# Window attention, forward and backward, on one core: the turn of P moved from TensorE to VectorE, three slots for turned y and h, and a new order of the first steps

## The chip, the cores and the metric

The kernel runs on one core of a Trainium2 chip. The metric is the time of one execution on the device in microseconds (us); for a set of runs the median is given. Engines: PE (TensorE, matmuls), DVE (VectorE), ACT (ScalarE), POOL (GpSimd) and SP (SyncE). POOL and SP do almost nothing here but issue DMAs.

## The reference

```python
def _fwd_reference(x, wqkv, wo):            # x (1, 256, 256, 384) bf16, C = 384
    # x is cut into 32 x 32 windows of 8 x 8 = 64 positions: xw (1024, 64, 384)
    qkv = xw @ wqkv
    q, k, v = qkv[..., :C], qkv[..., C:2*C], qkv[..., 2*C:]
    p = softmax(einsum('bqc,bkc->bqk', q, k) * C ** -0.5)
    o = einsum('bqk,bkc->bqc', p, v) @ wo
    return o                                 # windows put back in place

def reference(x, wqkv, wo, grad_out):
    out, vjp = jax.vjp(_fwd_reference, x, wqkv, wo)
    return (out, *vjp(grad_out))             # out, dx, dwqkv, dwo
```

## The kernel before

The weights are multiplied together first, so that q, k and v are never formed: A = scale wq wk^T and B = wv wo, with their transposes AT and BT. Then for each window y = x A, the scores are y x^T, and P is their softmax; h = grad_out BT, and h x^T is the gradient of P, from which D, the gradient of the scores, follows. out is P x B. dx is made of D x AT, D^T y and P^T h. For the weights only two sums over all windows are needed, x^T V with V = D^T x, and x^T W with W = P^T grad_out; an epilogue multiplies them by the weights.

**Units.** A quad is 8 windows, 512 positions, kept as four tiles t of 128 partitions with two windows (64 partitions each, w = 0, 1). There are NQ = 128 quads, and `step(n)` is called once for each. The order inside a step is written by hand: each engine runs its instructions in the order in which the code issues them, and waits by semaphores where data or a buffer isn't ready. A step works on several quads at once: n (attention products and outputs), n+1 (turn of P), S = n+2 (scores and softmax), A = n+3 (projections), n+4 (turns of inputs), n+5 (loads).

**Parts of a step, with their lines.** All matmuls go through a helper (L85), and ACT and DVE evictions from PSUM through `ev` (ACT L89, DVE L91).

- `md(n)`: x times the turned P and D (tile TT), 48 matmuls in 64x64 pieces, evicted to MD.
- a dW block (`Block.mms`): x^T V or x^T W for 24 tiles (six quads) and 128 of the 384 rows. In the two-bank form (banks 3 and 4) each tile takes four 64x64 matmuls of 384 columns, in the one-bank form (bank 3) one 128x128 matmul. Tiles 0 to i1 and i1 to i2 use two banks, i2 to the end one. `blk.add` adds a bank to ACC on DVE (L309) and so frees it.
- `attn2(n, h)`: V, W and two of the three parts of dx for half a quad, 64x64 pieces; it reads P and D (PB), x, grad_out and the turned y and h (YH). V and W are evicted to VW, with a slot for each of NVW quads. The steps before the first dW block is there (n = 0, 1, 2, called early) use `attn_vw` and other banks.
- `dxs(n, t)`: the third part of dx; `dxs_ev` evicts it to DXS on ACT, and POOL stores it (L277).
- `scores(S)`: both score products into bank 4, from HYS, in which `stack` (DVE, L134) has put y and h side by side.
- `chain0`, `chain2`, `chain3`: the softmax and its gradient. chain0 (DVE, L153 and L155) subtracts the maximum into SS, chain2 (ACT, L159) is the exponential, chain3 (DVE, L163 to L170) gives P and D in PB; it reads bank 4 again (L167), and after that the bank is free. UM is a buffer of chain3.
- `proj(A, 0)` and `proj(A, 1)`: y and h of a later quad, held transposed, evicted to YHT. They read the turned inputs XT and DOT.
- `outs(n, t0)`: out from MD and B, evicted to OS on ACT, stored by POOL (L219).
- `turn_p(n+1)`: P and D turned within each window: 16 PE transposes of 64x64 (L179) into bank 7, and one DVE copy to TT (L180).

**Turns and loads.** SP's queue issues, in this order in each step: the turns by DMA of x and grad_out of quad n+4 (`turn_in`, L111, to XT with three slots and DOT with two), the load of grad_out of quad n+5 (L107), and the turns of y and h of quad n+2 (`turn_yh`, L115, to YH with NTOK = 2 slots). POOL's queue loads x of quad n+5 (L103) and stores both outputs. ACT's queue issues DMAs at the start and the end only.

A prologue forms A, B, AT and BT (`wprod`), and brings quads 0 to 2 to where step 0 needs them.

Of the kernel before, what the change touches and what calls it, by code (L numbers as in the profile page):

```python
# [11 lines left out]
BF16 = mybir.dt.bfloat16  # L12
# [4 lines left out]
def kernel(  # L17
# [18 lines left out]
    NQ = (H // 16) * NQC  # L36
    scale = float(C) ** -0.5
    GQ = 6
    NX, ND, NXT, NDT, NYH, NTOK, NVW = 13, 5, 3, 2, 3, 2, 9

    def cut(q):

# [28 lines left out]
    SS = sb.tile([P, 4, 64], F32, name="SS")  # L71
    PEX = sb.tile([P, 4, 64], F32, name="PEX")
    TM = sb.tile([P, 4, 64], F32, name="TM")
    UM = sb.tile([P, 4, 64], F32, name="UM")
    ST = sb.tile([P, 4, 4], F32, name="ST")
    ACC = sb.tile([P, 2 * CK, C], F32, name="ACC")
    ident = sb.tile([P, P], BF16, name="ident")
# [6 lines left out]
    def mm(out, lhsT, rhs, start, stop):  # L84
        PE.matmul(out, lhsT=lhsT, rhs=rhs, start=start, stop=stop, skip_group_check=True)  # L85
# [28 lines left out]
    def turn_yh(n, a):  # L114
        SP.dma_start_transpose(out=YH[:, n % NTOK, a, :, :],  # L115
                               in_=YHT[:, n % NYH, a, :, :].rearrange("p m t -> p (m t)"))
# [14 lines left out]
    def stack(n, a, m0, m1):  # L131

        dst = HYS[:, 4 * m0:4 * m1, 0::3, :] if a == 0 else HYS[:, 4 * m0:4 * m1, 1:3, :]
        DVE.tensor_copy(out=dst, in_=YHT[:, n % NYH, a, m0:m1, :].rearrange("p m (t w k) -> p (m t) w k", w=2, k=64))  # L134
# [16 lines left out]
    def chain0(n):  # L151
        for w in range(2):
            DVE.tensor_reduce(out=ST[HALF[w], 0, :], in_=sd(w, w), axis=AX.X, op=ALU.max)  # L153
        for w in range(2):
            DVE.tensor_tensor(out=SS[HALF[w]], in0=sd(w, w),  # L155
                              in1=ST[HALF[w], 0, :].unsqueeze(2).to_broadcast([64, 4, 64]), op=ALU.subtract)

    def chain2(n):
        ACT.activation(out=PEX[:], in_=SS[:], func=ACTF.Exp)  # L159
# [10 lines left out]
        DVE.tensor_tensor(out=pb[:, 0], in0=TM[:], in1=UM[:], op=ALU.subtract)  # L170

    def turn_p(n):
        bb = PS[:, 7, 256:512].bitcast(BF16)
        for t in range(4):
            for a in range(2):
                for w in range(2):
                    r = slice(64 * w, 64 * w + 64)
                    o = t * P + a * 64
                    PE.transpose(bb[r, o:o + 64], PB[r, n % 2, a, t, :], ident[r, r])  # L179
        DVE.tensor_copy(out=TT[:, n % 2, :, :, :].rearrange("p t a k -> p (t a k)"), in_=bb)  # L180

    def pturn(dst, src, banks, engs):

# [88 lines left out]
    def dxs_ev(n, h, eng):  # L272
        ev(eng, DXS[:, n % 2, 2 * h:2 * h + 2, :].rearrange("p a c -> p (a c)"),
           PSF[:, DXB + 2 * h * C:DXB + 2 * h * C + 2 * C])
        for t in (2 * h, 2 * h + 1):
            for w in range(2):
                POOL.dma_start(out=img(out_1, n, t)[8 * w:8 * w + 8], in_=DXS[64 * (1 - w):64 * (1 - w) + 64, n % 2, t, :])  # L277

    class Block:
# [8 lines left out]
        def mms(self, banks, i0, i1):  # L288

            if i0 == 0:  # L290
                self.banks = len(banks)
            for i in range(i0, i1):
                q, t = self.tiles[i]
                s0, s1 = i == 0, i == len(self.tiles) - 1
                xs, vs = (q % NX) * 4 + t, (q % NVW) * 4 + t
                if len(banks) == 1:
                    mm(PS[:, banks[0], 0:C], X[:, xs, self.ma * P:(self.ma + 1) * P], VW[:, vs, self.which, :], s0, s1)
                    continue
                for hh in range(2):
# [42 lines left out]
    def wprod(dst, lt, r0, sc):  # L342
        for mo in range(CK):
            o = PS[:, bank[0] % 6, 0:C]
            bank[0] += 1
            for m in range(CK):
                mm(o, lt[:, m, mo * P:(mo + 1) * P], r0[:, m, :], m == 0, m == CK - 1)
            if sc:
                ACT.activation(out=dst[:, mo, :], in_=o, func=ACTF.Copy, scale=scale)
            else:  # L350
                DVE.tensor_copy(out=dst[:, mo, :], in_=o)

    def step(n):
        S, A = n + 2, n + 3
        doS, doA = S < NQ, A < NQ
        early = not todo
        if n + 4 < NQ:
            turn_in(n + 4, 0)
            turn_in(n + 4, 1)

        md(n)
        if early:
            if doA:
                proj(A, 0, (3, 4, 0, 5), (ACT, ACT, ACT, DVE))
            if n + 1 < NQ:
                turn_p(n + 1)
            attn_vw(n, 0, 0)
            vw_ev(n, 0, 0, ACT)
            attn_vw(n, 1, 2 * 512)
            attn_vw(n, 2, 2 * 512 + 2 * C)  # L370
            vw_ev(n, 1, 2 * 512, DVE)
            vw_ev(n, 2, 2 * 512 + 2 * C, ACT)
            attn_vw(n, 3, 0)
            vw_ev(n, 3, 0, ACT)
            if doS:
                stack(S, 0, 0, 3)
                stack(S, 1, 0, 3)
            if n + 5 < NQ:
                load_x(POOL, n + 5)
        else:  # L380
            blk = todo.pop(0)
# [48 lines left out]
        outs(n, 0, (5, 6), ACT)  # L430
        outs(n, 2, (4, 7) if early else (0, 1), ACT)
        outs_st(n)
        if not early and doA:
            proj(A, 1, (7, 2, 4, 3), (ACT, ACT, ACT, DVE))
        elif not doA:
            fill(7, 2, 4)

    def gate(ap):
# [2 lines left out]
    with tc.manual_schedule():  # L441
# [33 lines left out]
        wprod(A_sb, wT[:, 0:CK], wT[:, CK:2 * CK], True)  # L475
# [6 lines left out]
        wprod(BT_sb, wo_sb, wT[:, 2 * CK:3 * CK], False)  # L482
        stack(0, 0, 0, 3)
        pturn_in(1, 0, (6, 7), (ACT, ACT))
        proj(0, 1, (4, 5, 0, 1), (ACT, DVE, ACT, DVE))
        stack(0, 1, 0, 3)
        turn_yh(0, 1)
        turn_in(2, 1)
        pturn_in(1, 1, (6, 7), (ACT, ACT))
        scores(0)  # L490
        chain0(0)
        proj(1, 0, (0, 1, 2, 3), (ACT, ACT, ACT, ACT))
        turn_yh(1, 0)
        chain2(0)
        chain3(0)
        proj(1, 1, (5, 6, 7, 0), (ACT, ACT, ACT, ACT))
        turn_yh(1, 1)
        stack(1, 0, 0, 3)
        stack(1, 1, 0, 3)
        wprod(AT_sb, wT[:, CK:2 * CK], wT[:, 0:CK], True)  # L500
        scores(1)
        chain0(1)
        wprod(B_sb, wT[:, 2 * CK:3 * CK], wo_sb, False)
        turn_in(3, 0)
        turn_in(3, 1)
        turn_p(0)
        chain2(1)
        chain3(1)
        proj(2, 0, (0, 1, 4, 5), (ACT, ACT, ACT, ACT))
        proj(2, 1, (6, 7, 0, 4), (ACT, ACT, ACT, ACT))  # L510
        for n in range(NQ):
            step(n)
            if n == NQ - 3:
# [78 lines left out]
```

## Time and profile before

| | |
|---|---|
| median of 7 runs | 1965.92 us (1956.68 to 1990.76) |
| profiled execution, its own time | 1962.67 us |
| its span | 1960.8 us |
| PE, DVE, ACT, POOL busy | 99%, 69%, 69%, 58% of the span |
| step 0 begins | 38.0 us |
| granted TensorE clock | 0.999 |
| SP's turns of y and h, from issue to landing | 7.3 us (median) |
| the same for x, grad_out | 6.6 us, 8.9 us |

A row of the profile's groups or timeline names the line, the engine, the operation, output<-inputs, the tile (partitions x elements) and the time; in brackets stands the engine's idle time before it and what ended it. PE's 99% is time in which some matmul was under way; matmuls overlap, so the share alone doesn't say how fast they follow each other. The chain of waits is followed back from the last instruction: where it stays on PE, nothing but PE's own order held it up.

### The profile page before, as it was taken

To read this page: it belongs to the slowest core of one execution; us is meant where nothing else is said; L and a number is where in the kernel's file an instruction comes from. 1 tells how busy PE (TensorE), PEld (TensorE's weight loads), DVE (VectorE), ACT (ScalarE), POOL (GpSimd) and SP (SyncE) were. 2 spreads that over 40 slices of the span, in tenths; PEclk is the share of its full clock that TensorE was granted. 3 is DMA by queue.
4 is the path that set the end of the run, shared out by engine and by line. 5 is a ranking of instruction groups with operands and counts; after the bars stand their busy time and mean duration, and the time that the engine had idled before them with its cause. 6 is when DMAs were issued, how large, how long until landed. Compare 5 with 4: busy or idle time off the path is not lost.

```text
span 1960.8 us, 78332 instructions
## 1 busy us (share of the span) xinstructions
PE 1935.7 (99%) x32789; PEld 1351.8 (69%) x32789; DVE 1362.4 (69%) x2851; ACT 1353.0 (69%) x2204; POOL 1141.7 (58%) x2059
## 2 busy tenths in 40 slices
PE   8899999999999999999999999999999999999999
PEld 5576776776677677677667767766767667667766
DVE  5676777677677777767767777776666767767774
ACT  5777767766776776777677677677666777677664
POOL 3666556656655665665666565566555656566543
PEclk9999999999999999999999999999999999999999
DMA  9999999999999999999999999999999999999992
GB/s 211 203 217 218 214 220 211 212 220 210 217 221 204 220 219 205 215 212 219 219 213 219 210 207 214 218 206 218 206 199 213 212 218 216 203 217 225 211 178 75
DMA packets 972659, 410.12 MB, mean 209 GB/s; under 512 B 855312, under 2 KB 947280, under 8 KB 972304
## 3 DMA queue, kind: packets, MB, share of 16 engines
q1 hardware_dynamic: 872032, 252.05, 82.6%
q0 software_dynamic: 98496, 151.78, 30.5%
q8 instruction: 256, 4.19, 0.9%
q10 hardware_dynamic: 1776, 1.28, 0.2%
q14 instruction: 99, 0.81, 0.1%
HBM read 102.73 MB, written 101.84 MB: 104 GB/s over the span
## 4 chain that ended last, share of the span: by engine, by line
PE 96%; DMA 1%; DVE 1%; ACT 1%; issue 0%; ACTq 0%; SPq 0%; DVEq 0%
PE PS L85 94%; PE PS L179 2%; DMA YH<-YHT 1%; DMA DO<-in_grad_out_dram 0%; DMA X<-in_x_dram 0%; DVE TM L167 0%; ACT VW L89 0%; ACT YHT L89 0%; DVE SS L155 0%; DVE ST L153 0%; ACT DXS L89 0%; ACT VW L529 0%; ACT OS L89 0%; DVE PB L165 0%; DVE ST L163 0%
## 5 line engine op out<-in xcount | busy, mean ns | idle before, releaser
L277 POOL DMA_DIRECT2D out_dram<-DXS x1024 | 577.7, 571 | 599.7 <-ACT DXS L89 556.4
L85 PE MATMUL PS<-VW,X 64*64 64x384 bf16 (+1 forms) x8661 | 575.8, 325 | 0.0
L85 PEld LDWEIGHTS <-X 64*64 64x64 bf16 (+1 forms) x14805 | 435.9, 106 | 121.1 <-issue 23.9
L85 PEld LDWEIGHTS <-MD 128*128 128x128 bf16 x3840 | 343.3, 98 | 214.9 <-issue 30.9
L89 ACT CAST YHT<-PS 128x512 bf16<-128x512 f32 (+1 forms) x770 | 409.3, 553 | 15.9 <-PE PS L85 6.5
L89 ACT CAST VW<-PS 128x768 bf16<-128x768 f32 x384 | 294.6, 801 | 143.9 <-PE PS L85 143.8
L219 POOL DMA_DIRECT2D out_dram<-OS x512 | 273.8, 540 | 140.7 <-ACT OS L89 64.1
L103 POOL DMA_DIRECT2D X<-in_x_dram x508 | 285.9, 569 | 57.9 <-PE PS L85 36.9
L85 PE MATMUL PS<-AT_sb,MD 128*128 128x384 bf16 (+2 forms) x2304 | 294.2, 273 | 0.4 <-ACT DXS L89 0.4
L85 PE MATMUL PS<-B_sb,MD 128*128 128x384 bf16 x1536 | 271.5, 326 | 4.2 <-ACT DXS L89 2.1
L85 PE MATMUL PS<-XT,A_sb 128*128 128x512 bf16 (+1 forms) x1170 | 269.9, 376 | 2.9 <-DVE TM L167 1.8
L85 PE MATMUL PS<-DOT,BT_sb 128*128 128x256 bf16 (+1 forms) x1527 | 270.5, 327 | 0.0
L89 ACT CAST DXS<-PS 128x768 bf16<-128x768 f32 x256 | 204.5, 799 | 85.4 <-PE PS L85 76.9
L89 ACT CAST OS<-PS 128x768 bf16<-128x768 f32 x256 | 204.5, 800 | 77.2 <-PE PS L85 64.0
L91 DVE CAST MD<-PS 128x512 bf16<-128x512 f32 x384 | 241.3, 684 | 6.3 <-PE PS L85 6.3
L91 DVE CAST YHT<-PS 128x256 bf16<-128x256 f32 (+1 forms) x129 | 55.2, 429 | 260.5 <-PE PS L85 258.7
L85 PEld LDWEIGHTS <-BT_sb 128*128 128x128 bf16 x1527 | 149.2, 98 | 112.4
L89 ACT CAST MD<-PS 128x512 bf16<-128x512 f32 x384 | 200.2, 594 | 36.1 <-PE PS L85 36.1
L85 PE MATMUL PS<-YH,PB 64*64 64x256 bf16 (+2 forms) x3072 | 211.2, 270 | 4.6 <-DMA YH<-YHT 4.6
L159 ACT ACTIVATE PEX<-SS 128x256 f32<-128x256 f32 x128 | 53.3, 417 | 228.3 <-DVE SS L155 228.3
L85 PEld LDWEIGHTS <-PB 64*64 64x64 bf16 x6144 | 187.8, 107 | 24.9 <-issue 7.2
L309 DVE TENSOR_TENSOR ACC<-PS,ACC 128x384 f32<-128x384 f32 x254 | 140.6, 554 | 65.1 <-PE PS L85 64.8
(65 smaller groups left out, 1823.2 us busy)
## 6 DMA issues: line engine op xcount, KB each, us to landing
out_dram<-DXS POOLq DMA_DIRECT2D x1024, 48.0 KB
out_dram<-OS POOLq DMA_DIRECT2D x512, 96.0 KB
X<-in_x_dram POOLq DMA_DIRECT2D x508, 96.0 KB
DO<-in_grad_out_dram SPq DMA_DIRECT2D x504, 96.0 KB, 4.8
YH<-YHT SPq DMA_TRANSPOSE x256, 7.3
XT<-X SPq DMA_TRANSPOSE x126, 6.6
DOT<-DO SPq DMA_TRANSPOSE x126, 8.9
XT<-in_wqkv_dram SPq DMA_DIRECT2D x1, 864.0 KB
```

What stands on the lines that cost most here:

```text
L85: PE.matmul(out, lhsT=lhsT, rhs=rhs, start=start, stop=stop, skip_group_check=True)
L89: ACT.copy(out=out, in_=in_)
L91: DVE.tensor_copy(out=out, in_=in_)
L103: q.dma_start(out=X[:, (n % NX) * 4 + t, :], in_=img(x, n, t))
L159: ACT.activation(out=PEX[:], in_=SS[:], func=ACTF.Exp)
L179: PE.transpose(bb[r, o:o + 64], PB[r, n % 2, a, t, :], ident[r, r])
L219: POOL.dma_start(out=img(out_0, n, t), in_=OS[:, n % 2, t, :])
L277: POOL.dma_start(out=img(out_1, n, t)[8 * w:8 * w + 8], in_=DXS[64 * (1 - w):64 * (1 - w) + 64, n % 2, t, :])
L309: DVE.tensor_tensor(out=dst[:, self.k, :], in0=PS[:, bank, 0:C], in1=ACC[:, self.k, :], op=ALU.add)
```

## The change

- `turn_p` no longer uses PE or PSUM. DVE transposes PB in blocks of 32x32 into Z, a bf16 view of SS, copies the whole of it to TT in TT's order, and then overwrites the blocks off the diagonal of each window by four copies of 32 partitions that swap them. In the steps with a dW block it stands where it stood, between the two stretches of two-bank dW matmuls, but after both stacks; in the early steps it comes after the stacks instead of before `attn_vw`.
- YH has three slots instead of two, and `turn_yh(S)` is issued first in the step, ahead of the turns of x and grad_out of quad n+4.
- VW has eight slots instead of nine. UM is no longer a buffer of its own but SS.
- In the dW block i2 goes from 15 to 20, and the one-bank rest comes after all of `dxs`. Its last matmul is split into 128 and 256 columns.
- `dxs_ev(n, 1)` comes before chain2 on ACT, and `blk.add(3)` before chain3 on DVE.
- The early steps have an order of their own: both `dxs_ev` first, then scores, `outs` in banks 1, 2 and 5, 6 between the parts of the softmax, and `proj(A, 1)` last.
- In the prologue the banks of `wprod` are given one by one, and the turns, stacks, scores and projections of quads 0 to 2 are in another order.

```diff
-    NX, ND, NXT, NDT, NYH, NTOK, NVW = 13, 5, 3, 2, 3, 2, 9
+    NX, ND, NXT, NDT, NYH, NTOK, NVW = 13, 5, 3, 2, 3, 3, 8
...
-    UM = sb.tile([P, 4, 64], F32, name="UM")
+    UM = SS
+    Z = SS[:].rearrange("p t k -> p (t k)").bitcast(BF16)
...
     def turn_p(n):
-        bb = PS[:, 7, 256:512].bitcast(BF16)
-        for t in range(4):
-            for a in range(2):
-                for w in range(2):
-                    r = slice(64 * w, 64 * w + 64)
-                    o = t * P + a * 64
-                    PE.transpose(bb[r, o:o + 64], PB[r, n % 2, a, t, :], ident[r, r])
-        DVE.tensor_copy(out=TT[:, n % 2, :, :, :].rearrange("p t a k -> p (t a k)"), in_=bb)
+        zz = Z.rearrange("p (a t k) -> p a t k", a=2, t=4)
+        DVE.transpose(out=Z, in_=PB[:, n % 2].rearrange("p a t k -> p (a t k)"))
+        DVE.tensor_copy(out=TT[:, n % 2], in_=zz.rearrange("p a t k -> p t a k"))
+        for w in range(2):
+            for i in range(2):
+                r, o = 64 * w + 32 * i, 64 * w + 32 - 32 * i
+                DVE.tensor_copy(out=TT[o:o + 32, n % 2, :, :, 32 * i:32 * i + 32],
+                                in_=zz[r:r + 32, :, :, 32 - 32 * i:64 - 32 * i].rearrange("p a t k -> p t a k"))
...
                 if len(banks) == 1:
-                    mm(PS[:, banks[0], 0:C], X[:, xs, self.ma * P:(self.ma + 1) * P], VW[:, vs, self.which, :], s0, s1)
+                    for c in (slice(0, P), slice(P, C)) if i == 23 else (slice(0, C),):
+                        mm(PS[:, banks[0], c], X[:, xs, self.ma * P:(self.ma + 1) * P], VW[:, vs, self.which, c], s0, s1)
...
         early = not todo
+        if doS:
+            turn_yh(S, 0)
+            turn_yh(S, 1)
         if n + 4 < NQ:
             turn_in(n + 4, 0)
             turn_in(n + 4, 1)
...
-            if n + 1 < NQ:
-                turn_p(n + 1)
             attn_vw(n, 0, 0)
...
                 stack(S, 1, 0, 3)
+            if n + 1 < NQ:
+                turn_p(n + 1)
...
-            i1, i2 = (7, 15) if nb == 4 * GQ else (nb // 2, nb)
+            i1, i2 = (7, 20) if nb == 4 * GQ else (nb // 2, nb)
             blk.mms((3, 4), 0, i1)
             attn2(n, 0, (ACT, ACT))
             if doS:
                 stack(S, 0, 0, 3)
+                stack(S, 1, 0, 3)
             if n + 1 < NQ:
                 turn_p(n + 1)
-            if doS:
-                stack(S, 1, 0, 3)
             blk.mms((3, 4), i1, i2)
...
-        if doS:
-            turn_yh(S, 0)
-            turn_yh(S, 1)
...
             dxs_ev(n, 0, ACT)
-            blk.mms((3,), i2, nb)
         dxs(n, 3)
         dxs(n, 2)
         if early:
             dxs_ev(n, 0, ACT)
+            dxs_ev(n, 1, ACT)
             if doS:
                 scores(S)
                 chain0(S)
+            outs(n, 0, (1, 2), ACT)
+            if doS:
+                chain2(S)
+            outs(n, 2, (5, 6), ACT)
+            outs_st(n)
+            if doS:
+                chain3(S)
+            if doA:
+                proj(A, 1, (1, 0, 3), (ACT, ACT, ACT))
+            return
+        blk.mms((3,), i2, nb)
+        dxs_ev(n, 1, ACT)
         if doS:
             chain2(S)
-        dxs_ev(n, 1, ACT)
+        blk.add(3)
         if doS:
             chain3(S)
-        if not early:
-            blk.add(3)
         if doA:
-            proj(A, int(early), (0, 1, 2), (ACT, ACT, ACT))
+            proj(A, 0, (0, 1, 2), (ACT, ACT, ACT))
...
         proj(0, 1, ...)
         stack(0, 1, 0, 3)
-        turn_yh(0, 1)
         turn_in(2, 1)
+        turn_yh(0, 1)
         pturn_in(1, 1, (6, 7), (ACT, ACT))
         scores(0)
+        turn_in(3, 0)
         chain0(0)
...
```

More of the change, by code (lines that the diff above doesn't have):

```diff
@@ L340, with wprod @@
     bank = [0]
-    def wprod(dst, lt, r0, sc):
+    def wprod(dst, lt, r0, sc, banks):
         for mo in range(CK):
-            o = PS[:, bank[0] % 6, 0:C]
-            bank[0] += 1
+            o = PS[:, banks[mo], 0:C]
             for m in range(CK):
@@ L430, in step @@
         outs(n, 0, (5, 6), ACT)
-        outs(n, 2, (4, 7) if early else (0, 1), ACT)
+        outs(n, 2, (0, 1), ACT)
         outs_st(n)
-        if not early and doA:
+        if doA:
             proj(A, 1, (7, 2, 4, 3), (ACT, ACT, ACT, DVE))
-        elif not doA:
+        else:
             fill(7, 2, 4)
@@ L474 @@
             wturn(j, DVE if j % 2 == 0 else ACT)
-        wprod(A_sb, wT[:, 0:CK], wT[:, CK:2 * CK], True)
+        wprod(A_sb, wT[:, 0:CK], wT[:, CK:2 * CK], True, (0, 1, 2))
+        bank[0] = 3
         for j in range(2 * CK, 3 * CK):
@@ L481 @@
         turn_in(2, 0)
-        wprod(BT_sb, wo_sb, wT[:, 2 * CK:3 * CK], False)
+        wprod(BT_sb, wo_sb, wT[:, 2 * CK:3 * CK], False, (0, 1, 2))
         stack(0, 0, 0, 3)
         pturn_in(1, 0, (6, 7), (ACT, ACT))
-        proj(0, 1, (4, 5, 0, 1), (ACT, DVE, ACT, DVE))
+        proj(0, 1, (4, 5, 0), (ACT, DVE, ACT))
         stack(0, 1, 0, 3)
+        turn_in(2, 1)
         turn_yh(0, 1)
-        turn_in(2, 1)
         pturn_in(1, 1, (6, 7), (ACT, ACT))
         scores(0)
+        turn_in(3, 0)
         chain0(0)
-        proj(1, 0, (0, 1, 2, 3), (ACT, ACT, ACT, ACT))
-        turn_yh(1, 0)
+        proj(1, 0, (1, 2, 3), (ACT, ACT, ACT))
         chain2(0)
         chain3(0)
-        proj(1, 1, (5, 6, 7, 0), (ACT, ACT, ACT, ACT))
-        turn_yh(1, 1)
+        turn_p(0)
+        proj(1, 1, (5, 6, 7), (ACT, ACT, ACT))
+        turn_in(3, 1)
+        wprod(AT_sb, wT[:, CK:2 * CK], wT[:, 0:CK], True, (1, 2, 3))
         stack(1, 0, 0, 3)
         stack(1, 1, 0, 3)
-        wprod(AT_sb, wT[:, CK:2 * CK], wT[:, 0:CK], True)
+        wprod(B_sb, wT[:, 2 * CK:3 * CK], wo_sb, False, (5, 6, 0))
+        turn_yh(1, 0)
+        turn_yh(1, 1)
         scores(1)
         chain0(1)
[L503 to L506, printed above, removed]
+        proj(2, 0, (5, 2, 1), (ACT, ACT, ACT))
         chain2(1)
         chain3(1)
-        proj(2, 0, (0, 1, 4, 5), (ACT, ACT, ACT, ACT))
-        proj(2, 1, (6, 7, 0, 4), (ACT, ACT, ACT, ACT))
+        proj(2, 1, (7, 6, 3), (ACT, ACT, ACT))
         for n in range(NQ):
```

## The prediction

> **What bounds the kernel now.** I read the page's first rows, then the chain that ended last, then the engines' timelines over one step, and last SP's own queue.
>
> ```profile
> PE 1935.7 (99%) x32789; PEld 1351.8 (69%) x32789; DVE 1362.4 (69%) x2851; ACT 1353.0 (69%) x2204; POOL 1141.7 (58%) x2059
> ```
>
> PE has no idle time to speak of, so a step costs what PE has to stream. The chain between 895 and 928 us shows two whole steps:
>
> ```profile
> 897.66 0.18 PE PS L179 x11
> 897.84 0.01 PE PS L85
> 897.85 0.06 PE PS L179 x4
> 897.92 14.62 PE PS L85 x226
> 912.53 0.18 PE PS L179 x11
> ```
>
> A step is 912.53 - 897.66 = 14.87 us; the turns of P on PE (L179) take 0.25 of it, the other matmuls 14.62. The step's first matmuls (the MD products) start at 909.88; offsets below (+x) count from there. DVE in that step:
>
> ```profile
> 912.21 0.55 DVE L134 COPY HYS<-YHT 128x1536 bf16<-128x1536 bf16 x1
> 912.82 0.42 DVE L180 COPY TT<-PS 128x512 bf16<-128x512 bf16 x1
> 913.16 0.63 DVE L134 COPY HYS<-YHT 128x1536 bf16<-128x1536 bf16 x1
> 914.14 0.56 DVE L309 TENSOR_TENSOR ACC<-PS,ACC 128x384 f32<-128x384 f32 x1 [0.35 <-PE PS L85]
> 915.39 0.96 DVE L91 CAST VW<-PS 128x768 bf16<-128x768 f32 x1 [0.70 <-ACT VW L89]
> ```
>
> DVE is busy for 10.5 us of a step. A second stream is nearly as full as PE. SP's queue, issue by issue:
>
> ```profile
> 898.84 4.80 SPq L115 DMA_TRANSPOSE YH<-YHT  x2
> 903.86 2.14 SPq L111 DMA_TRANSPOSE XT<-X  x1
> 906.22 2.00 SPq L111 DMA_TRANSPOSE DOT<-DO  x1
> 908.27 2.94 SPq L107 DMA_DIRECT2D DO<-in_grad_out_dram  x4
> 911.31 5.16 SPq L115 DMA_TRANSPOSE YH<-YHT  x2
> ```
>
> Each issue begins within 0.3 us of the end of the one before, here and through the run. A cycle took 12.47 us here and 16.04 the next time. From the pair at 140.33 to the pair at 1869.91 are 116 cycles, 14.91 us each, against PE's 14.87. SP runs late: counted back from the last pair (1903.48, step 125), the pair at 1869.91 is that of step 122, which began at 1854.3, so it goes out 15.6 us after its step began, though its slot was free at about +5. When SP slips further, PE stops:
>
> ```profile
> 1418.92 8.72 PE PS L85 x110
> 1427.64 8.14 DMA YH<-YHT
> 1435.82 0.44 PE PS L85 x5
> ```
>
> There PE waited 2.3 us for turned y and h. All such stalls of this execution come to 7.6 us (steps over 14.87 near 1401, 1436, 1468 and 1780). So PE is the bound by a hair, and SP's turns are next.
>
> **The change, part by part.**
>
> *PE turns of P removed.* 16 transposes a step, 0.25 us of PE. L179 is 1.6% of the chain, 31 us. In the 117 steps after the start-up that is 117 x 0.25 = 29 us off PE.
>
> *DVE turns instead.* A transpose of 128x512, a copy of 128x512 and four copies of 32x256; removed is the 0.42 us copy L180. No row shows the transpose. The DVE rows give a slope: casts of 512 and 768 elements take 684 and 958 ns, about 1.05 ns an element over some 150 ns fixed; HYS moves 1536 bf16 elements in 550, a quarter of that slope. Transpose: 0.28 us if it ran as HYS does, [...] I take 0.68, [...] nearest to the casts [...]. Copies at the HYS slope: 0.28 and 4 x 0.22; at the slow slope 0.69 and 4 x 0.42. Five gaps add 0.15. Sum 2.0 us, bounds 1.6 and 3.6. DVE goes to about 12.1 us of a step: still no bound.
>
> What waits is the path behind it. Both stacks now come first; without the L180 copy they end at +3.5, the turn at +5.5, the add that frees bank 4 at +6.05. Scores need bank 4 at +6.36: before +5.79 (915.67), plus five dW tiles at 0.163 us (seven took 910.57 to 911.71), less 0.25. Slack 0.3 us, so the turn costs nothing up to 2.3 us; past that each 0.1 us costs about 12 us of run. MD of the next step reads the turn 9 us later.
>
> [...] Trace first: HYS copies take 547 to 550 ns, at worst 667, with POOL issuing beside them. [...] By the row, five times 0.12 is 0.6 at worst and about nothing usually. I use 0.05, which the slack hides. [...] The rows' 150 ns decide.
>
> *Five dW tiles moved from the one-bank stretch (L85, 128x128) to the two-bank stretch (64x64).* 0.163 against 0.162 us a tile: nothing. The split last tile adds one matmul and one weight load, between 0 and 0.05 us; dxs streams 128- and 256-column pieces without a gap, so 0.01. The remaining four tiles come after dxs, 0.65 us, and the add that frees bank 3 is covered by the exponential. DXS's second copy no longer waits for the exponential on ACT: off PE's path, worth nothing, but its eight POOL stores start earlier.
>
> *Eight VW slots, UM and Z in SS.* The slot rewritten by a step belongs to the oldest quad, whose tiles its dW block reads in the seven tiles ahead of attn2: PE's own order covers it. SS is written again only after the exponential has read it. Both cost nothing.
>
> *Turns of y and h first in the step, three slots.* SP's cycle is still YH YH XT DOT DO, so its throughput stays. What moves is slack. The YH pair goes one step ahead of XT and DOT, so YH is no longer first to be late. XT and DOT of quad n+4, and the load of DO, now stand behind a pair that needs the last piece of y and h from DVE at +0.5. Their readers are proj at about +8.8 and +12.7 in the next step. With XT issued as late as now (+8 to +11), landing in 6.6 us (DOT 8.9), proj has some 7 to 8 us left; YH had 4 to 5. A small gain in slack; the risk is that SP now waits at the start of a step if it ever catches up.
>
> *First steps reordered.* In steps 0 to 2 PE waits behind DXS, scores' chain and OS (14.7 us a step for some 12.6 of PE). The new order takes bank 4 out of that way, up to 2 us in each of three steps, 6 us. But SP needed 15.4 us a cycle there (91.61 to 106.99), and XT and DOT for the next proj stand behind YH. When PE next ran at 13.08 a step, SP fell 9 us behind in three steps. So: between -6 and +5, I take 0.
>
> *Sum.* SP's mean cycle is 14.91 and PE would run at 14.62, so some steps will stall. Cycles range from 12.5 to 17 and were shortest when YH went out some 18 to 20 us after its step, so SP can follow a faster PE part of the time. I charge 9 us of further stalls: 1962.7 (span 1960.8 and 1.9 around it) - 29 + 9 = 1943. The median shown is 3.2 above that execution: 1946.
>
> **The rivals.**
>
> A, the forecast: PE's 0.25 us is kept for two thirds; 1946 (1925 to 1955). For it: PE 99% busy, shorter SP cycles than needed do occur. Chance 0.42.
>
> B, SP sets the pace: SP's cycle stays 14.91 whatever PE does, PE's gain turns into waits for XT, DOT or YH. For it: no gap in SP's queue over 1700 us, six of seven runs lie over the stall-free 1955 (1962.7 - 7.6). Against: PE alone would not be at 99% if SP were the longer one. The time is that of now less the 4 us by which SP was ahead at the end: 1962 (1950 to 1975). Chance 0.30, of it faster 0.08, same 0.18, slower 0.04.
>
> C, slower: XT and DOT late at proj. They queue behind the pair in every step; once PE is held at proj, SP stays in the slow cycles of 16.1 and 16.3 us seen at 1424 to 1457, where it was late before. It decides from a mean cycle over 14.95. At 15.1 (the slowest run shown, 1990.8, fits that) the run takes 124 x 0.2 = 25 us longer: 1990. Chance 0.16.
>
> D, DVE late: the turn takes 3 us because the copies get the slow slope; scores wait 0.7 us a step, 0.45 more than was saved, 117 x 0.45 = 53 us: 2018. At 2.55 us it is even. The HYS row speaks against it. Chance 0.12.
>
> That the turn leaves PE altogether is sure from the order of instructions; it isn't a rival.
>
> **How the numbers follow.** A measurement of this kernel can tell about 0.5%, 10 us, from no change: faster is below 1956, slower above 1976. Faster 0.42 + 0.08 = 0.50; same 0.18; slower 0.04 + 0.16 + 0.12 = 0.32. The range runs from all of the 31 us and the first steps' 6 with few stalls (1925, less 3 for noise) to C's 1990; A's own is 1925 to 1955.
>
> **What would show it.** Right: L179 gone, the chain's PE pieces 14.6 us long, a transpose near 0.68 us and small copies near 0.22, scores without a wait for ACC. Rival B or C: waits of PE for DMA XT, DOT or YH totalling over 25 us, SP still without gaps, cycle 14.9 or more. D: PE waiting for DVE ACC ahead of scores, copies over 0.35 us. The forecast is wrong if the steps in mid-run aren't below 14.8.

## The result, and the profile after

The changed kernel takes 1995.44 us (median of 12 runs, 1974.11 to 2003.28) against 1970.52 of the kernel before beside it (31 runs). The ratio is 1.0128 with a 95% interval of 1.0095 to 1.0161: slower, by 25 us, where 1946 was forecast. A second set of runs gave 2005.61 and 1.016 (1.0105 to 1.0214). The profiled execution took 2001.5 us, its span 1999.7.

The first row of the page, engine by engine:

```profile
PE 1920.3 (96%) x32664; PEld 1296.9 (65%) x32664; DVE 1541.8 (77%) x3490; ACT 1365.7 (68%) x2200; POOL 1136.6 (57%) x2059
```

PE has less to do than before (1935.7) and is no longer busy all the time. The timeline of DVE over one step shows the turn of P at its new place:

```profile
899.03 1.03 DVE L135 COPY HYS<-YHT 128x1536 bf16<-128x1536 bf16 x2
899.98 0.69 DVE L176 STREAM_TRANSPOSE SS<-PB 128x512 bf16<-128x512 bf16 x1
900.71 0.29 DVE L177 COPY TT<-SS 128x512 bf16<-128x512 bf16 x1
901.03 0.92 DVE L181 COPY TT<-SS 32x256 bf16<-32x256 bf16 x4
901.98 0.56 DVE L312 TENSOR_TENSOR ACC<-PS,ACC 128x384 f32<-128x384 f32 x1
```

From 899.98 to 901.95 the turn takes 1.97 us, and nothing waits for it. That an unstalled step is shorter is seen where the chain of waits stays on PE for nearly 100 us; the row of the transposes in that window (smallest, median and largest duration in ns, first and last start) gives its length:

```profile
1196.22 98.48 PE PS L86 x1629
```
```profile
L176 DVE STREAM_TRANSPOSE SS<-PB x7: 691/692/701, 1207.1 to 1294.8; 128x512 bf16<-128x512 bf16 x7
```

Seven transposes are six steps: (1294.8 - 1207.1) / 6 = 14.62 us. But such stretches are rare. The chain between 880 and 960 us, where before it ran on PE alone:

```profile
880.00 1.68 PE PS L86 x26
881.67 9.05 DMA XT<-X
890.72 0.04 issue
890.76 6.58 PE PS L86 x66
897.34 8.41 DMA XT<-X
905.75 0.04 issue
905.79 53.59 PE PS L86 x902
959.38 9.31 DMA DOT<-DO
```

Followed back from its end, the run hangs again and again on the landing of turned x or grad_out. The shares of the chain, first before and then after:

```profile
PE 96%; DMA 1%; DVE 1%; ACT 1%; issue 0%; ACTq 0%; SPq 0%; DVEq 0%
```
```profile
PE 71%; DMA 24%; DVE 1%; ACT 0%; issue 0%; DVEq 0%; ACTq 0%
```

The waits of PE (total us, times, longest):

```profile
PE PS L86 <- DMA XT<-X: 58.9, 46, 3.6
PE PS L86 <- DMA DOT<-DO: 3.2, 6, 0.8
```

Before, waits for DMA turns were 5.3 us, all for YH:

```profile
PE PS L85 <- DMA YH<-YHT: 4.6, 3, 2.3
PEld L85 <- DMA YH<-YHT: 0.7, 1, 0.7
```

SP's queue in the changed kernel around 900 us:

```profile
891.21 5.91 SPq L116 DMA_TRANSPOSE YH<-YHT  x2
897.34 1.93 SPq L112 DMA_TRANSPOSE XT<-X  x1
899.49 3.28 SPq L112 DMA_TRANSPOSE DOT<-DO  x1
902.82 3.38 SPq L108 DMA_DIRECT2D DO<-in_grad_out_dram  x4
906.30 5.99 SPq L116 DMA_TRANSPOSE YH<-YHT  x2
```

It has no gap over 0.45 us (median 0.08; before: none over 0.57, median 0.10), but a cycle is longer: from the pair at 126.10 to the pair at 1900.27 are 116 cycles, 15.29 us each, where it was 14.91. Step 7 begins at 131.4 us (before: 136.2) and step 124 at 1923.4 (before: 1884.1). So the start-up won 5 us (3 of them in the prologue: step 0 begins at 34.9 instead of 38.0), and the 117 steps between lost 44.

Below, "the pair's place" is the time from the start of a step's MD products to the issue of SP's pair of YH turns within that step. It is 8 to 11 us through most of this run. In the kernel before, the pair went out 16 to 20 us after its step began in most steps, so 2 to 5 us into the following one. "Step" and "mean step" (of steps 7 to 124, if nothing else is said) are read from the trace, from one step's first MD product to the next one's; an "unstalled" step is one without a wait of PE.

### The profile page after: what moved, and what is told of

Its sections match the earlier page's. It is cut to its first block, busy times and chain, and to the rows that moved or that the text cites. A ratio compares the mean times of both kernels' runs of the same rounds, so it can differ in the third digit from the quotient of the medians.

```text
span 1999.7 us, 78708 instructions
## 1 busy us (share of the span) xinstructions
PE 1920.3 (96%) x32664; PEld 1296.9 (65%) x32664; DVE 1541.8 (77%) x3490; ACT 1365.7 (68%) x2200; POOL 1136.6 (57%) x2059
## 3 DMA queue, kind: packets, MB, share of 16 engines
q1 hardware_dynamic: 872032, 252.05, 83.4%
q0 software_dynamic: 98496, 151.78, 32.2%
## 4 chain that ended last, share of the span: by engine, by line
PE 71%; DMA 24%; DVE 1%; ACT 0%; issue 0%; DVEq 0%; ACTq 0%
PE PS L86 71%; DMA XT<-X 20%; DMA DOT<-DO 3%; DVE MD L92 0%; ACT VW L90 0%; ACT VW L541 0%; ACT DXS L90 0%; DVE HYS L135 0%; DVE TT L181 0%; DVE SS L156 0%; DVE ST L154 0%; DVE SS L176 0%; DVE ACC L314 0%; DVE ACC L312 0%; PE PS L551 0%
## 5 line engine op out<-in xcount | busy, mean ns | idle before, releaser
L86 PE MATMUL PS<-VW,X 64*64 64x384 bf16 (+3 forms) x10599 | 562.9, 321 | 0.0
L86 PEld LDWEIGHTS <-MD 128*128 128x128 bf16 x3840 | 335.8, 98 | 196.6 <-issue 30.5
L86 PE MATMUL PS<-XT,A_sb 128*128 128x512 bf16 (+1 forms) x1164 | 276.5, 383 | 61.0 <-DMA XT<-X 58.9
L104 POOL DMA_DIRECT2D X<-in_x_dram x508 | 278.0, 554 | 56.3 <-PE PS L86 34.9
L86 PEld LDWEIGHTS <-A_sb 128*128 128x128 bf16 x1164 | 114.1, 99 | 181.1 <-issue 77.3
L86 PEld LDWEIGHTS <-PB 64*64 64x64 bf16 x6144 | 173.3, 107 | 33.9 <-issue 5.8
```

The costliest lines, as they stand in the source:

```text
L104: q.dma_start(out=X[:, (n % NX) * 4 + t, :], in_=img(x, n, t))
```

## The experiments

Theory 1 was at first that the new order of SP's queue costs the slack, theory 2 that the queue can't do a step in less than about 15 us whatever its order, theory 3 that DVE's block copies slow the queue. The kernel before ran beside each set of runs, at 1968 to 1973 us; each ratio below is to it.

### One part undone, or one part alone

**e1.** The changed kernel with the pair behind the load of grad_out again:

```diff
-        if doS:
-            turn_yh(S, 0)
-            turn_yh(S, 1)
         if n + 4 < NQ:
...
             load_do(SP, n + 5)
+        if doS:
+            turn_yh(S, 0)
+            turn_yh(S, 1)
```

> The changed kernel with one part undone: the turns of y and h stand behind the turns and the load of the inputs again, as before; everything else is as changed. Theory 1 (order: XT and DOT behind the YH pair are late at proj, and that wait is the whole loss): waits of PE for XT fall from 58.9 us to under 5, waits for YH stay under 15, time 1940 to 1955, ratio to before 0.985 to 0.993. Theory 2 (SP's stream is at its limit whatever the order: a faster PE only turns into waits): waits move from XT to YH, 25 us or more of them, ratio 0.995 to 1.01. Theory 3 (the DVE copies of the turn get in the way of POOL's issues and so of the transfers): SP's cycle stays at 15.3 us, ratio 1.01 or more.

Measured: 2006.43 us, but the six times spread from 1930 to 2028, too far for a ratio. In the trace, of an execution of 2020 us, the waits of PE are now for YH:

```profile
PE PS L86 <- DMA YH<-YHT: 57.6, 77, 1.9
PEld L86 <- DMA YH<-YHT: 28.2, 28, 2.0
```

The new order is not the whole cause; theory 1 falls. One run took 1930 us. With steps of 14.62 throughout, and start and end as in the trace, it would have been about 1918 (an estimate), so there can have been few stalls in it, and the queue *can* follow a step of 14.62. That run left no trace; e12 shows the same with one. That spoke against theory 2 in its plain form, and led to the next theory.

**e2.** The kernel before with the pair first (NTOK 3, NVW 8), all else as it was.

> The kernel before with only the turns of y and h moved to the front of the step, three slots for them and eight VW slots; P is still turned on PE. Theory 1: PE waits for XT as in the changed kernel, SP's cycle about 15.3 us, ratio 1.008 to 1.02. Theory 2: PE at 14.87 a step asks less of SP, waits of 10 to 20 us, ratio 0.995 to 1.005. Theory 3: no DVE turn, so no harm: ratio 0.99 to 1.0.

Measured: 1977.53 us, ratio 1.0058 (1.0032 to 1.0085).

```profile
PE PS L85 <- DMA XT<-X: 13.6, 15, 2.4
PE PS L85 <- DMA DOT<-DO: 2.0, 3, 1.1
```

The order alone, with its three slots, makes waits for x and grad_out at PE's old pace, and costs 0.6%. The pair's place is 8 to 10 us and the mean step 15.06.

**e3.** The kernel before with DVE's turn of P alone (i2 stays at 15, the turn between the two stacks).

> The kernel before with only the turn of P on DVE (same place, i2 = 15, order of SP's queue and slots as before; UM and Z in SS). Theory 1: PE's step is 14.62 us, SP's order is the old one, ratio 0.985 to 0.993. Theory 2: PE waits for YH for 25 us or more, ratio 0.995 to 1.01. Theory 3: SP's cycle 15.2 us or more, ratio over 1.01.

Measured: 1977.27 us, ratio 1.0055 (1.003 to 1.0079).

```profile
PE 63%; DVE 33%; issue 3%; ACT 1%; DVEq 0%; ACTq 0%
```
```profile
PE PS L86 <- DVE ACC L311: 7.7, 37, 0.3
```

No waits for a DMA turn, so theory 3 isn't borne out here: the copies run, and the queue keeps to 14.98, with the pair mostly 14 to 18 us after its step began. A third of the chain lies on DVE: scores wait for the add that frees bank 4, on the path that rival D had named, and the unstalled step is 14.97. The changed kernel has five more dW tiles ahead of scores and both stacks ahead of the turn, and has no such wait: there scores begin 6.35 us into a step (forecast 6.36) and the add ends at 5.84. Which of the moves does it was not tested one by one.

**e4.** The changed kernel with the load of grad_out issued by POOL (`load_do(POOL, n + 5)`).

> The changed kernel with the four loads of grad_out in each step issued by POOL instead of SP; SP issues only the four turns. It asks whether SP's own issue time or the transfers set SP's cycle. If issue time: the cycle loses the 2.5 us of the four loads, PE no longer waits for XT, ratio 0.985 to 0.993. If the transfers: the turns take that much longer each, the cycle stays over 14.8 us and the ratio is 0.997 to 1.015.

Measured: 2164.11 us, ratio 1.1011 (1.0966 to 1.1055). On POOL the loads of grad_out waited for slots that PE had yet to read (134 us in all), and the stores of dx stood behind them (98.0 us until such a load had landed); PE waited for DXS:

```profile
PE PS L86 <- ACT DXS L90: 170.5, 98, 5.3
```

Nothing follows for SP's cycle. As a remedy it is out.

### Pace, traffic and place

e1's one fast run suggested that what a cycle of SP costs depends on where in PE's step its turns fall. Three things could be varied: PE's pace, the other traffic, and the place.

**e5.** e1 and three products of 200 columns on constants:

```diff
+            for i in range(3):
+                mm(PS[:, 7, 256:456], ident[:], A_sb[:, i, 0:200], True, True)
             blk.mms((3, 4), i1, i2)
```

> The changed kernel with the two turns of y and h moved back behind the load of grad_out (as in e1), and three matrix products of 200 columns (constant operands, result unused) put on TensorE in the dW stretch where the turns of P stood: about 0.25 us more of TensorE work in each step, so that its unstalled step is 14.87 us again instead of 14.62. The result of the kernel is not touched. Theory 'TensorE has become faster than SyncE's queue': the queue keeps up again as it did before the change, the waits for YH and XT fall from 86 us to under 15 us, and the time is 1955 to 1970: more TensorE work makes the kernel faster than e1 (2006). Theory 'VectorE's block copies slow the queue': SyncE's cycle stays at 15.3 to 15.5 us and the time at 1995 to 2010. Theory 'the queue's order and early steps have put it in a place from which it doesn't come back': as the second, since nothing moves it back.

Measured: 1986.7 us (1983.53 to 1996.01), ratio 1.0104 (1.0054 to 1.0153). There are hardly any waits left:

```profile
PE 93%; DMA 2%; DVE 1%; issue 0%; ACT 0%; DVEq 0%; ACTq 0%
PE PS L86 <- DMA YH<-YHT: 3.8, 3, 2.6
```

but the unstalled step is 15.11 us, not 14.87: 600 columns added 0.49 instead of 0.25. From step 24 on the mean is 15.20, so the queue follows at that pace. Of the 20 us to e1 a part may be its spread.

**e8.** The changed kernel without the stores of dx in every second step, so that half of dx is missing from its output:

```diff
+                if n % 2:
                     POOL.dma_start(out=img(out_1, n, t)[8 * w:8 * w + 8], ...
```

> The changed kernel without the stores of dx in every even step: this leaves out half of the stores of dx, 192 KB per step on average, which are GpSimd's. TensorE, VectorE and ScalarE do what they did. Theory 'capacity, shared with the stores': SyncE's cycle falls below TensorE's 14.62 us, no waits for XT, time 1935 to 1950. Theory 'issue time of SyncE alone' (each entry costs what it costs, whatever else moves): cycle 15.2 to 15.3, time 1985 to 2000.

Measured: 1947.22 us (1926.82 to 1970.45), ratio 0.9844 (0.9805 to 0.9882). The profiled execution took 1930 us, with a mean step of 14.71 and

```profile
PE PS L86 <- DMA XT<-X: 3.3, 2, 2.8
```

SP issued exactly the same entries, and its mean cycle fell from 15.29 to 14.65. So the cycle's length isn't SP's own issue time alone: POOL's stores lengthen it. The page shows what the two queues share, the 16 DMA engines: they are 90% busy or more in every slice of the span but the last, before and after the change, and the packets of SP's queue (252 MB) took 83.4% of the engines' time in the changed kernel, those of POOL's (152 MB) 32.2%.

**e6.** A product of 64 columns that reads the turned x of step n+3 early, so that PE, and with it everything else, is held there rather than 6 us later at the projection:

```diff
+            if doA:
+                mm(PS[:, 7, 256:320], XT[:, A % NXT, 0, :], XT[:, A % NXT, 11, 0:64], True, True)
             blk.mms((3, 4), i1, i2)
```

> The changed kernel with one product of 64 columns more per step on TensorE, placed in the dW stretch some 2.5 us into the step, that reads the turned x of step n+3 (result unused): TensorE asks for that turn about 6 us earlier than the projection does, so that it is held there and not later, and the turns of SyncE's queue are issued that much earlier against TensorE's step. Theory 'the queue's cycle depends on where in TensorE's step its turns fall' (14.9 us in the kernel before, with the pair of y and h going out 2 to 3 us into a step; 15.3 to 15.5 us where they go out 8 to 9 us into one): SyncE's cycle falls to 14.7 to 14.9 us and the time to 1935 to 1960. Theory 'capacity' (the queue can't do a step in less than 15.1 to 15.3 us beside this traffic, wherever it falls): cycle 15.3, time 1990 to 2010, with the waits moved from the projection to the new product.

Measured: 1968.84 us, ratio 1.0000 (0.9969 to 1.0031): 27 us faster than the changed kernel. The pair's place is now mostly 1 to 3 us, and from step 24 on the mean step is 14.90. But the unstalled step was 14.88: the 64 columns had cost 0.26, so pace and place were mixed. DMA has 3% of e6's chain, where it had 24% in the changed kernel:

```profile
PE 93%; DMA 3%; DVE 1%; ACT 0%; issue 0%; DVEq 0%; ACTq 0%
```

**e7.** The same for e1, reading YH of the next step ahead of the last projection (`mm(PS[:, 7, 0:64], YH[:, (n + 1) % NTOK, 1, 0, :], YH[:, (n + 1) % NTOK, 1, 11, 0:64], True, True)`).

> As e1 (the turns of y and h last), with one product of 64 columns per step on TensorE, ahead of the last projection some 12.7 us into the step, that reads the turned y of the next step (result unused): TensorE asks for it some 4 us before the attention products do, so that the queue is held about 4 us earlier against TensorE's step than in e1. Theory 'where in the step': cycle 14.7 to 14.9 us, time 1935 to 1960. Theory 'capacity': cycle 15.4 to 15.5, time 1995 to 2015, the waits moved to the new product.

Measured: 1967.32 us (22 runs, 1956.08 to 1984.15), ratio 0.999 (0.9963 to 1.0017). The unstalled step is 14.65 and the mean one 15.05, between the two expectations. e1's spread is gone with it.

**e9.** e6 with a 64x64 product, the shape of its neighbours:

```diff
+            if doA:
+                mm(PS[0:64, 7, 256:320], XT[64:128, A % NXT, 0, 0:64], XT[64:128, A % NXT, 11, 0:64], True, True)
             blk.mms((3, 4), i1, i2)
```

> As e6, but the small product that reads the turned x of step n+3 is a 64x64 one like the dW and attention products around it, not a 128x128 one. In e6 the step came out at 14.88 us, 0.26 more than in the changed kernel, for a product of 64 columns; in e5 three of 200 columns cost 0.49 instead of 0.25. Theory 'a product of another array shape between 64x64 ones costs TensorE about 0.24 us': the unstalled step falls to 14.65 us. Theory 'SyncE's cycle depends on where in the step its turns fall': held at 1 to 3 us into the step, the queue follows this too with few waits, and the time is 1935 to 1955, below the kernel before. Theory 'e6 was unstalled only because its step was 14.88': waits of 30 to 60 us for XT at the small product, mean step 14.85 to 15.05, time 1960 to 1980.

Measured: **1943.19 us** (six runs, 1940.61 to 1948.39), ratio 0.9864 (0.982 to 0.9908). The unstalled step is 14.65, the mean one 14.78, the pair's place 1 to 5 us. This beats the kernel before by 28 us and the changed kernel by 52. PE waited for XT 12 us in all, 7 of them once, in step 6, which took 24.5 us and after which the pair goes out as early as it can:

```profile
PEld L86 <- DMA XT<-X: 12.1, 9, 7.1
PE PS L86 <- DMA XT<-X: 9.5, 4, 6.9
```

(PEld and PE here are largely the same stalls, seen at the weight load and at the matmul.)

**e10.** The changed kernel with e5's useless products in the 64x64 shape, 0.25 us a step, and no hold:

```diff
+            for i in range(3):
+                mm(PS[0:64, 7, 256:456], ident[64:128, 64:128], A_sb[64:128, i, 0:200], True, True)
```

> The changed kernel with three 64x64 products of 200 columns (constant operands, result unused) on TensorE in the dW stretch: 0.25 us more work per step, step 14.87 us as before the change, and nothing that holds TensorE earlier. Theory 'the queue's place in the step decides': the pair of y and h still goes out 8 to 9 us into the step, cycle 15.0 to 15.1 as in e2, waits for XT of 14 to 25 us, time 1968 to 1980, so that 31 us of useless work make the changed kernel 15 to 25 us faster. Theory 'capacity alone': the cycle stays at 15.3, time 1993 to 2000.

Measured: 1968.12 us (14 runs), ratio 0.9996 (0.996 to 1.0033). More work on PE makes the changed kernel 27 us faster, as the first theory said; "capacity alone" falls. Its detail was wrong: the pair didn't stay at 8 to 9 us. It began at 10 to 12 us in steps 5 to 10 (mean of steps 7 to 24: 15.67), and by step 30 had moved to 1 to 4, where the mean step was 14.9.

**e11.** The control to e9: the same small product, reading `ident` and `A_sb` instead of XT.

> As e9, but the small 64x64 product reads constants instead of the turned x, so that TensorE does the same work and is held by nothing earlier than in the changed kernel. Theory 'it is the hold, and with it the place of the turns in the step, that made e9 faster': as the changed kernel, 1985 to 2000, waits for XT at the projection of 45 to 65 us, SyncE's mean cycle 15.25 to 15.35. Theory 'any small addition to TensorE's order does it': as e9, 1940 to 1950.

Measured: 1969.96 us (14 runs, 1951.46 to 1985.22), ratio 0.9986 (0.9942 to 1.0029). Neither expectation was met: e9's hold is worth some 25 us over this (27 by the medians, 24 by the ratios), but this is already some 25 us under the changed kernel, though it holds nothing. Its trace shows why the times spread. The chain between 700 and 860 us is that of the changed kernel, and after 1150 us it is PE's alone:

```profile
701.32 10.78 DMA XT<-X
712.10 0.04 issue
712.14 5.85 PE PS L86 x32
717.99 9.68 DMA XT<-X
...
767.44 8.24 DMA XT<-X
```
```profile
1499.96 100.19 PE PS L86 x1722
```

One program, one execution: steps 24 to 60 take 15.29 us with the pair at 8 to 11 us; between steps 67 and 72 the pair moves to 0 to 4 us; steps 84 to 122 take 14.66, PE's own length. The queue has two places here, and stays for a long time in either. SP's issues in the late place, and in the early one:

```profile
791.37 5.61 SPq L116 DMA_TRANSPOSE YH<-YHT  x2
797.20 2.31 SPq L112 DMA_TRANSPOSE XT<-X  x1
799.73 3.53 SPq L112 DMA_TRANSPOSE DOT<-DO  x1
803.30 2.51 SPq L108 DMA_DIRECT2D DO<-in_grad_out_dram  x4
```
```profile
1502.41 6.29 SPq L116 DMA_TRANSPOSE YH<-YHT  x2
1508.91 2.50 SPq L112 DMA_TRANSPOSE XT<-X  x1
1511.63 2.48 SPq L112 DMA_TRANSPOSE DOT<-DO  x1
1514.16 2.91 SPq L108 DMA_DIRECT2D DO<-in_grad_out_dram  x4
```

The turn of grad_out differs most: 3.30 us to issue on average between 300 and 1000 us, 2.46 between 1250 and 1850. POOL's stores of dx go out 8 to 12 us into a step in both. In the late place they meet the pair, and the turn of grad_out meets the loads of x; in the early place they meet the turns of x and grad_out, and the pair meets the loads of x.

### Pushing the queue from one place to the other

**e12.** e9's hold in the steps before step 24 only (`if doA and n < 24:`).

> As e9, but with the holding product only in the steps before step 24. Theory 'the good place keeps itself once it is reached' (the start-up's fast steps are what pushed the queue out of it): 1938 to 1955, few waits for XT after step 24. Theory 'without the hold the queue slips back to 8 us into the step and stays there': mean step of the last 80 steps 15.2 to 15.3, time 1975 to 1992.

Measured: 1948.1 us (six runs: 1933, 1936, 1939, 1958, 1961, 1965), ratio 0.9883 (0.9808 to 0.9958). In the profiled one the chain from 463 us to the last steps is two pieces of PE, 1396 us without a wait:

```profile
463.48 731.22 PE PS L86 x12400
1194.69 0.18 issue
1194.88 665.22 PE PS L86 x11207
```

The pair stays at 0.5 to 5.6 us over steps 62 to 122 without being held. So the queue is fast enough for a step of 14.62, once it is early. The other three runs are 20 to 30 us longer. That would fit a queue that slipped, but it isn't shown: there is no trace of them.

**e13.** The changed kernel again, beside e14 to e16.

> The changed kernel itself, as it is, run again beside e14 to e16 on one chip. Theory 'two places': it starts in the late one and mostly stays there: 1985 to 2003, some runs 10 to 20 us shorter where the queue finds the early place on its way. Theory 'the added product of e11 is what helps': 1990 to 2003, no shorter runs.

Measured: 2005.61 us (1991.76 to 2012.36), ratio 1.016 (1.0105 to 1.0214): no shorter runs, pair at 7 to 13 us over steps 62 to 122, mean step 15.30. In 18 runs of the changed kernel the lowest is 1974, while e11 has a median of 1970. Why a product on constants of 0.03 us makes it so much likelier that the queue gets early isn't settled.

**e14.** e12, with the turn of x issued five times in step 60:

```diff
-            turn_in(n + 4, 0)
+            for k in range(5 if n == 60 else 1):
+                turn_in(n + 4, 0)
             turn_in(n + 4, 1)
```

> As e12 (hold in the steps before step 24 alone), but in step 60 the turn of x is issued five times instead of once (same source, same slot), which makes SyncE's queue about 10 us later once, or up to 28 us if each waits for the one before to land. Theory 'two places, each keeps itself': steps 24 to 60 at 14.65 us, then TensorE is held at the projection by 4 to 22 us once, and after it the queue stays 8 us or more into the step with a cycle of 15.1 to 15.3 for most of the rest: 20 to 40 us more than e12 (1948), 1965 to 1990. Theory 'e12 was fast for another reason': the delay costs its 4 to 22 us and the steps after it are 14.65 again at once.

Measured: 1987.14 us (19 runs), ratio 1.0044 (1.0009 to 1.0078), 39 us over e12 by the medians and 32 by the ratios. The turns waited for each other (7.38, 7.63, 4.43, 3.64 and 3.81 us in the chain, one after the other), and PE stood once:

```profile
936.83 7.38 DMA XT<-X
...
963.83 36.24 PE PS L86 x521
```

Step 61 took 28.9 us instead of 14.6. After it the pair's place was 7 to 9 us, where it had been 2 to 5. The next twelve steps still took 14.62; then the stalls came, and steps 62 to 122 have a mean of 15.08 with the pair at 7 to 13 us to the end. Without any lasting change to the program the late place kept itself here for the 60 steps that were left. It need not do so for good: in e10 and e11 the queue left it after some 15 and 60 steps.

**e15.** The same push with the hold in every step (e9).

> As e9 (hold in every step), with the same four turns more in step 60. Theory 'two places': TensorE is held once at the small product, by about as much as the queue was delayed (10 to 28 us), and the steps after that are 14.65 to 14.8 again: 1950 to 1972. Theory 'the hold does nothing but its wait': steps of 15.1 to 15.3 after step 60 as in e14.

Measured: 1966.67 us (22 runs), ratio 0.9976 (0.9952 to 1). Step 61 took 31.7 us; in step 62 the pair is back at 2.2, and steps 62 to 122 have a mean of 14.77, as steps 24 to 60 had. The hold brings the queue back at the price of one wait (15.3 us, and about 1.7 more, an estimate, of the step in which the granted clock was 0.5).

**e16.** e9's product ahead of `attn2(n, 1)`, 2 us later in the step.

> As e9, but the holding product stands behind the two-bank dW matmuls, 2 us later in the step. Theory 'two places': it lets the queue be 2 us later, still earlier than the projection does; fewer waits while the queue is early, weaker pull back: 1938 to 1960. If the border between the two places lies between 5 and 7 us into the step, 1960 to 1985.

Measured: 1951.18 us (1947.2 to 1955.13), ratio 0.9893 (0.9851 to 0.9934). From step 20 on the place is nearly that of e9, and there is no gain over it.

## Why the prediction was wrong

**What held.** "PE turns of P removed": the unstalled step is 14.62, as forecast. "DVE turns instead": 1.97 us against 2.0, transpose 0.69 against 0.68, small copies 0.22 against 0.22, the whole copy 0.29 against 0.28, and scores don't wait. The upper bound of 3.6 is an estimate (1.2 us for a transpose at twice the casts' 1.05 ns an element, and the copies at the slow slope); it had left out its gaps (with them it is 3.7), which changed nothing. For the copies the forecast had gone by two rows of the profile, and both held. As the row of HYS had it (547 to 550 ns, at worst 667), POOL's issues lengthen the copies little: the 512 small ones have a median of 220 ns and a longest of 323, with POOL busy 57% of the span; the 146 that met an issue of POOL have a median of 222, and none of the others took over 225. And the fixed cost that follows from the copies' medians (294 ns for 512 elements, 220 for 256) is 146 ns, an estimate on a straight line through the two, against the 150 of the rows. e3, without the moved dW tiles and stacks, makes scores wait (7.7 us for ACC in 37 waits), so the slack ahead of scores came with the new order.

**The step that failed: "Turns of y and h first in the step, three slots", with its "A small gain in slack".** Right in it was that the turns of x and grad_out fall behind the pair; wrong was "so its throughput stays": SP's entries and their order are the same, but its mean cycle went from 14.91 to 15.29 us, with the pair now 8 to 11 us into a step. By e2 the new order alone puts the pair at 8 to 10 us and gives 16 us of waits; the other waits came with the faster PE and the new start-up. The 7 to 8 us of room at the projection were measured with the queue in its early place, and the working of the forecast didn't ask whether it would still be there.

**The "Sum".** "I charge 9 us of further stalls" was the term that was mis-sized. Steps 7 to 124 were to take 117 x 14.62, the 8 us of stalls there were, and 9 more: 1728 us. They took 1792.0, so the term was 64 too small. Of that, 62.1 us are PE's named waits for XT and DOT; less the 17 allowed, 45. The other 19 us don't stand in the waits, as PE counts as busy in them, but the trace shows most of them. In five steps (25, 37, 76, 103, 120) the granted clock was 0.5 for 3.4 us at the end of a wait, and the step is 1.78 to 1.85 us longer than 14.62 us and its wait; half of the 3.4 us (an estimate) is 1.7 us each, 8.5 in all. And each of the 52 waits lengthened its step by some 0.16 us more than the gap, 8 in all. Set against 5 us won by step 7, this makes up the 59 us between the 1943 worked out and the 2001.5 of the profiled execution.

**"First steps reordered", taken as 0.** PE's part came out at the good end: steps 0 to 2 took 4.3 us less. The text had also seen that SP falls behind there. Its price is not local: by step 5 the pair was at 9.5 us in the changed kernel. e12 undoes this one slip by a hold in the first 24 steps, and the run is 47 us shorter than the changed kernel's. But e11's product, which holds nothing, brings 25 of these by itself, and why is open; the hold's own part is some 22 us. So the price of the slip in the start-up was paid in the later steps.

**Rival C is what happened,** with the mechanism as it was told: XT and DOT late at the projection, PE held there, the queue kept in slow cycles. Its cycle was too short (15.1 assumed, 15.29 measured), and that its time of 1990 lies so near to 1995 is in part luck: it charged 25 us, where the two profiled executions differ by 39. It had a chance of 0.16. The remark in "Sum" that cycles "were shortest when YH went out some 18 to 20 us after its step" was the key: it says that the cycle's length depends on the place. The trace of before bears it out (a pair at 18 to 20 us was followed by a cycle of 14.57 us on average, one at 16 to 18 by 14.90), and so does the changed kernel's (15.28 for a pair at 8 to 10). It was used to argue that SP could follow; the other half, that a queue out of that place has longer cycles and is then held there by PE's own waits, belonged to rival C's chance.

**Shown, and not shown.** Shown, each by one traced execution: two places within one program (e11, e14), the early one fast enough for 14.62 (e12), the late one kept for 60 steps without a cause that lasts (e14), a hold that brings the queue back (e15), and POOL's stores as part of the cycle's length (e8). Not shown: which meeting of transfers costs the half microsecond or more of the late place; from one step to the next it is uneven (twelve steps of 14.62 in it after the push in e14). Not shown either is why the late place is dearer in the changed kernel (mean step 15.32) than in e2 (15.06), where PE is slower. Whether DVE's copies have a part in that is open: e3 tested them with the queue in its early place only.

## What to carry to other kernels

Here a DMA queue was nearly as full as the busiest engine (cycles of 14.91 us against steps of 14.87), and its cycle was no constant (15.29 us on average with the pair mostly 8 to 11 us into a step, where e12's queue followed steps of 14.62 with it at 0.5 to 5.6). In such a case read the cycle against the place in the engine's step at which the queue's entries fall, and before shortening that engine's step or its start-up ask where the queue will then stand and what holds it there. In the changed kernel the projection waited late (52 waits, 62.1 us) and the queue stayed at 8 to 11 us; a tiny product that asks for the data early set the place instead (1 to 5 us in e9), and turned a change that lost 25 us into one that gains 28, though about half of that came with a product of the same size that asks for nothing (e11). And first steps that are too fast for the queue can cost more later than they win: here they and the prologue won 5 us by step 7, and the hold in the first 24 steps alone was worth some 22 (an estimate from e11 and e12).

## What the hardware showed that was not expected

- 128x128 products put between 64x64 ones cost PE about 0.23 us a step beyond their columns: 600 columns made the step 0.49 us longer in 128x128 form (e5) and 0.25 in 64x64 form (e10); 64 columns 0.26 (e6) against 0.03 (e9). Among other 128x128 products the same 64 columns cost 0.03 (e7).
- Taking half of dx's stores away from another engine's queue (e8) shortened SP's mean cycle from 15.29 to 14.65 us, about PE's own 14.62, with SP's own entries unchanged.
- Some waits of PE cost more than themselves. In the changed kernel the granted clock was 0.5 for 3.4 us at the end of five waits of 2.1 to 3.6 us, as between 605.8 and 609.2 us, and their steps were 1.78 to 1.85 us longer than an unstalled step and the wait; other waits as long (2.8 us in step 30) had nothing of the kind.
- The same program ran in two regimes, 15.29 and 14.66 us a step in one execution (e11), with the same instructions in the same order on every engine.
